# Nine chunks turned by TensorE, mask selections on GpSimd, and a rebuilt order in a gated-attention and feed-forward kernel

## The chip, the cores and the metric

The kernel runs on one core of a Trainium2 chip. Its time is the device time of one execution in microseconds. Five engines work on it, each through its own queue in order: TensorE (PE in the profile; its weight loads are PEld), VectorE (DVE), ScalarE (ACT), GpSimd (POOL) and SyncE (SP), which issues all DMAs here.

## What is computed

A gated linear attention runs over 768 steps for 4 batches of 8 heads of width 48; its outputs are the 3072 tokens of a feed-forward layer with a hidden width of 2048. The weights come as 64-bit floats.

```python
state = np.zeros((B, H, D, D), dtype=np.float32)
for t in range(S):
    state = alpha[:, :, t, :, None] * state + np.einsum('bhd,bhe->bhde', k[:, :, t], v[:, :, t])
    y[:, :, t] = np.einsum('bhd,bhde->bhe', q[:, :, t], state)
x = y.transpose(0, 2, 1, 3).reshape(B * S, H * D)
h = x @ w_in
g = np.where(h >= 1, h, np.where(h <= -1, 0.0, (h + 1) ** 2 / 4))
out = g @ w_out
```

## The kernel before

**Tiling.** The tokens are cut into 24 chunks of 128 (numbered from 0, six to a batch), and the chunks into eight groups of three. Attention works by chunk, the feed-forward layer by group. The 2048 hidden columns are 16 tiles of 128 (`f`); the weights of two tiles are a pair `u`, so there are eight pairs.

**Preparing a chunk** (`prepare`). Alpha, k and q are brought into a form with the head width on partitions ("turned"). For chunks below `EARLY` they are loaded as they lie, 192 KB each, and TensorE turns them into a bank of PSUM (L521); for the others four DMAs of 96 KB per tensor load them in a form that VectorE transposes (L534) into a tile `turn` in SBUF. From the turned alpha VectorE makes two scans, `Q` forward (L610) and `inv` backward (L636), after scaling four columns (L601). Then `inv` is multiplied by the turned k (L654) and `Q` by the turned q (L660). GpSimd does the latter for chunks below `HELP`, after ScalarE has copied the turned q out of PSUM (L658), and for chunks from `EARLY` on; VectorE does it for those between.

**Attending a chunk** (`attend`, `begin_chunk`, `follow`). TensorE transposes the K product (L681), makes scores (L696) and state updates (L709) in two banks of PSUM. The scores are masked in two halves, into `Q` and into `other` (L781 on VectorE). For chunks below `HELP` the second half is copied by ScalarE (L754) and multiplied by the mask on GpSimd (L760). VectorE adds the updates into the state (L736, L738). Then TensorE makes the outputs (L835), and ScalarE and VectorE write them as a high and a low part into `ring` (L859, L864). From chunk 7 on, the outputs of a chunk come right behind the scores of the next. From group 1 on, six DMAs move parts within `ring` (L880).

**The feed-forward layer** (`hidden`, `second`). For a group and a tile `f`, nine matmuls make the hidden values (L931); VectorE clips them (L975), ScalarE squares (L960), VectorE takes the maximum (L986), ScalarE and GpSimd split the result in a high and a low part (L990, L991), and nine matmuls multiply it with the second weights (L1009). Nine matmuls of L931 or of L1009 are called a block here; there are 256. The first two groups run over half of the tiles each, then over the other half; their partial sums go to memory and back.

**Decoding the weights** (`decode`). Each of the 16 weight tiles of 128x768 is made from its 64-bit form by two ScalarE passes (L354, L362), two on VectorE (L370, L381), an addition (L393) and, after a ScalarE copy (L404), a subtraction (L405). The last two may go to GpSimd or VectorE.

**The order** is set by `Plan.order`: every instruction has a duration and a due time (`key`), and an estimate of when its engine, operands and buffers are free; the planner takes them one after the other and so fixes each engine's queue, and which of two engines takes an instruction that has two ways. A chunk's due time is `due`, `MARGIN` ahead of the blocks that need it; loads are due `LOAD` and weight loads `FETCH` ahead, decodings `DECODE`. Where TensorE would wait in the first `WARMTH` us, the planner puts in filling matmuls (L1080), which compute nothing. Attention has three of the eight banks of PSUM from chunk `ROOM` on; the chunks below may use `FIRST`.

Of the kernel before, what the change touches and what calls it, by code (L numbers as in the profile page):

```python
# [15 lines left out]
ALU = mybir.AluOpType  # L16
# [11 lines left out]
SHARE = 2  # L28
EARLY = 7
MORE = 2  # L30
WARM = 20
LAG = 3.0
FETCH = 12.0
LOAD = 8.0
DECODE = 4.0
PREPARE = 2.5
MARGIN = 9.0
AHEAD = 12.0
FIRST = 6
ROOM = 4  # L40
LATER = 8.0
MERGE = 6
WARMTH = 60.0
HELP = 3
VHELP = 6
SPLIT = 0
CLIPS = 6.0
NEAR = 0.25

# [22 lines left out]
class Plan:  # L72
# [57 lines left out]
    def order(self):  # L130
        free = dict.fromkeys(("PE", "DVE", "ACT", "POOL", "SP"), 1.0)
        slots = {name: [(0.0, -i, None) for i in range(n)] for name, (n, share, _) in self.sizes.items() if share == name}
# [8 lines left out]
        ready = {}  # L141
# [3 lines left out]
        mode, wire, done, freed = None, 0.0, [], 0  # L145
# [81 lines left out]
def gated_attention_ffn(ctx: ExitStack, tc: tile.TileContext, q, k, v, alpha, w_in, w_out, out):  # L227
    nc = tc.nc
# [73 lines left out]
    with ExitStack() as main:  # L302
# [116 lines left out]
        def weights(u):  # L419
# [7 lines left out]
            size = P * NW * DM * (8 if wide else 4)  # L427
            fetch = key - FETCH
            for r in range(2):
# [31 lines left out]
            wo[u] = make([P, 2, NW, DM], F32R)  # L461
            decode(u, "i", ti, wi[u], "p k f -> p (k f)", key - DECODE)
            decode(u, "o", to, wo[u], "p j m -> p (j m)", key - DECODE + LAG)

# [12 lines left out]
        def load(x, j, key):  # L477
            b, t0 = j // PER, j % PER * CH
            t, rows = raws[x], {"a": alpha, "k": k, "q": q}[x][b, :, t0 : t0 + CH, :]
            if j < EARLY:  # L480
                if j < 2:
                    plan.op("POOL", 0.15, -99, lambda: nc.gpsimd.memset(whole(t, j)[:, :, D:], 1.0), [], [(x, j % 2)])
                plan.op(
# [28 lines left out]
        def turned(x, j, key, to=()):  # L512

            t = raws[x]
            if j < EARLY:
# [10 lines left out]

                flips[j] = plan.op("PE", 0.45, key, flip, [(x, j % 2)], [ps, *to], mode="full", after=[flips[j]] if j in flips else [])
                return ps, view
# [16 lines left out]
        def prepare(j, key):  # L545
# [109 lines left out]
            qt, qT = turned("q", j, key + 0.2)  # L655
            if j < HELP:
                qs = buf("tp", "turn", [P, G * CH], 2)
                plan.op("ACT", 0.55, key + 0.2, lambda qT=qT: nc.scalar.copy(out=qs(), in_=qT()), [qt], [qs])  # L658
                qt, qT = qs, lambda: qs()
            mul = lambda e: e.tensor_tensor(out=flat(Q()), in0=flat(Q()), in1=qT(), op=ALU.mult)  # L660
            in_ps = HELP <= j < EARLY
            ways = [("DVE", 0.66, lambda: mul(nc.vector), not in_ps), ("POOL", 1.3, lambda: mul(nc.gpsimd), True)]
# [78 lines left out]
        def follow(j, key):  # L741
# [5 lines left out]
            for r, to in enumerate((Q, other)):  # L747
                for u in range(2):
                    if r and j < HELP:
# [9 lines left out]
                        if u:  # L759
                            cut = lambda e: e.tensor_tensor(  # L760
                                out=other()[0:HC].rearrange("p g (u t) -> p g u t", u=2),
                                in0=other()[0:HC].rearrange("p g (u t) -> p g u t", u=2),
                                in1=mask[0:HC, None, None, 0:HC].broadcast_to([HC, G, 2, HC]),
                                op=ALU.mult,
                            )
                            plan.op(
                                "POOL",
                                1.35,
                                key,
                                lambda: cut(nc.gpsimd),  # L770
                                [other],
                                [other],
                                port=True,
                                other=("DVE", 0.66, lambda: cut(nc.vector), True),
                            )
# [311 lines left out]
        for j in range(NCH):  # L1087
            n = max(n for n in range(NG) if first[n] <= j)
            since = begin[n - 1] if n > 0 else begin[n] - AHEAD
            due = since + (begin[n] - since) * (j - first[n] + 1) / groups[n] - MARGIN  # L1090
            prepare(j, due - PREPARE)
# [175 lines left out]
```

## Time and profile before

| | us |
|---|---|
| median of 3 runs (540.56 to 541.62) | 541.18 |
| the profiled execution | 542.22 |
| its span, first to last instruction | 540.4 |
| TensorE busy | 516.0 |
| VectorE busy | 399.3 |
| GpSimd busy | 276.0 |
| ScalarE busy | 265.5 |
| matmuls of L931 / L1009 / L1080 | 1152 / 1152 / 149 |

The page's slices show TensorE at nine tenths or more in every slice from 160 us on, and lower before. So the views that are used are those of the first 170 us. A row names the line, the engine, the operation and its tiles (out<-in); "idle before" is how long the engine stood idle and what released it.

### The profile page before, as it was taken

The page shows a single profiled execution, that of the slowest core. Times are in us where ns is not written, and L with a number is a line of the kernel's source. Part 1 is how long each engine was busy: PE and PEld are TensorE (multiplying, and loading weights), DVE is VectorE, ACT ScalarE, POOL GpSimd, SP SyncE. Part 2 cuts the span into 40 slices and gives each one's busy share as a digit, 9 for nine tenths or more (in the row PEclk, how much of TensorE's full clock was granted, in tenths as well). Part 3 has the DMA queues.
Part 4 walks back from the last instruction along what each step waited for, and adds up shares of the span by engine and source line. Part 5 has one row for each costly group of instructions (what it writes and reads, how often), then busy time and mean ns, then how long its engine had stood idle before and what let it go on. Part 6 is the DMA issues. An engine that isn't in the chain of part 4 may idle for free.

```text
span 540.4 us, 12713 instructions
## 1 busy us (share of the span) xinstructions
PE 516.0 (95%) x4923; PEld 494.9 (92%) x4923; DVE 399.3 (74%) x709; ACT 265.5 (49%) x490; POOL 276.0 (51%) x295
## 2 busy tenths in 40 slices
PE   8898979998589999999999999999999999999995
PEld 6787869987589999999999999999999999999995
DVE  4789889899988987967968887777787884334332
ACT  4668877676343444344354453444444544333332
POOL 7555888799955525425524543443543543233330
PEclk9989998999989999999999999999999999999999
DMA  9989699934044663334333444335324300101001
GB/s 178 196 173 225 146 210 197 268 74 118 7 111 134 146 154 90 87 79 122 86 77 96 102 105 106 100 61 140 96 45 116 90 16 3 22 1 44 2 0 49
DMA packets 109457, 55.05 MB, mean 102 GB/s; under 512 B 71536, under 2 KB 104272, under 8 KB 109392
## 3 DMA queue, kind: packets, MB, share of 16 engines
q1 hardware_dynamic: 109392, 54.19, 43.2%
q8 instruction: 40, 0.66, 0.5%
q14 instruction: 25, 0.20, 0.1%
HBM read 46.20 MB, written 5.90 MB: 96 GB/s over the span
## 4 chain that ended last, share of the span: by engine, by line
PE 79%; DVE 12%; issue 3%; ACT 2%; POOL 2%; DMA 1%; SPq 0%; DVEq 0%; ACTq 0%; POOLq 0%
PE ps L1009 33%; PE ps L931 33%; PE ps L835 5%; PE ps L709 2%; PE ps L681 2%; DVE w L381 2%; PE ps L1080 2%; PE ps L696 2%; DVE Q L610 2%; DVE inv L636 1%; DVE w L370 1%; DVE meet L649 1%; POOL wt L405 1%; DVE inv L654 1%; DVE gf L986 1%
## 5 line engine op out<-in xcount | busy, mean ns | idle before, releaser
L991 POOL TENSOR_TENSOR gh<-gf,gh 128x384 fp32r<-128x384 f32 x127 | 146.7, 1160 | 162.4 <-ACT gh L990 133.3
L1009 PE MATMUL ps<-wt,gh 128*128 128x384 f32 x1152 | 226.2, 341 | 2.1 <-POOL gh L991 2.1
L931 PE MATMUL ps<-ring,wt 128*128 128x384 f32 x1152 | 226.1, 343 | 1.9 <-POOL wt L405 1.8
L931 PEld LDWEIGHTS ps<-ring,wt 128*128 128x128 f32 x1152 | 205.3, 190 | 3.6 <-POOL wt L405 2.5
L1009 PEld LDWEIGHTS ps<-wt,gh 128*128 128x128 f32 x1152 | 202.9, 189 | 4.3 <-POOL gh L991 3.7
L960 ACT ACTIVATE gf<-gf,half_b 128x384 f32<-128x384 f32 x122 | 75.0, 616 | 114.3 <-DVE gf L975 90.9
L975 DVE TENSOR_SCALAR gf<-ps 128x384 f32<-128x384 f32 x122 | 67.0, 551 | 58.8 <-PE ps L931 50.1
L990 ACT CAST gh<-gf 128x384 fp32r<-128x384 f32 x128 | 65.7, 513 | 74.5 <-DVE gf L986 60.5
L986 DVE TENSOR_TENSOR gf<-gf,ps 128x384 f32<-128x384 f32 x128 | 70.0, 549 | 33.8 <-ACT gf L960 33.3
L728 ACT COPY both<-state 48x192 f32<-48x192 f32 x65 | 22.7, 350 | 45.4 <-POOL state L812 39.8
L405 POOL TENSOR_TENSOR wt<-w,wt 128x768 fp32r<-128x768 f32 x16 | 33.8, 2114 | 4.3 <-ACT wt L404 4.2
L393 POOL TENSOR_TENSOR w<-w,wt 128x768 int32<-128x768 int32 x14 | 27.4, 1960 | 10.1 <-DVE w L381 5.6
L660 POOL TENSOR_TENSOR Q<-Q,turn 128x512 f32<-128x512 f32 x20 | 25.8, 1292 | 7.2 <-DVE turn L534 5.9
L835 PE MATMUL ps<-other,both 128*64 128x64 f32 x372 | 27.9, 225 | 1.6 <-issue 1.5
L812 POOL TENSOR_TENSOR state<-state,last 128x192 f32<-128x192 f32 x20 | 11.3, 567 | 33.5 <-DVE state L738 33.4
L835 PE MATMUL ps<-Q,both 128*64 128x64 f32 x372 | 28.0, 226 | 0.1
L610 DVE TENSOR_TENSOR_SCAN Q<-turn,fwd 128x512 f32<-128x512 f32 x17 | 23.2, 1362 | 6.5 <-PE ps L835 6.4
L835 PEld LDWEIGHTS ps<-Q,both 128*64 128x64 f32 x372 | 24.0, 137 | 3.6 <-issue 1.5
L681 PE MATMUL ps<-ident,inv 128*128 128x128 f32 x96 | 15.2, 282 | 10.8 <-DVE inv L654 10.4
L781 DVE TENSOR_TENSOR Q<-ps,mask 64x256 f32<-64x256 f32 x48 | 20.3, 423 | 6.8 <-ACT other L746 5.3
L835 PEld LDWEIGHTS ps<-other,both 128*64 128x64 f32 x372 | 23.9, 137 | 1.1 <-issue 0.8
L681 PEld LDWEIGHTS ps<-ident,inv 128*128 128x128 f32 x96 | 11.7, 144 | 13.1 <-DVE inv L654 11.1
(89 smaller groups left out, 525.9 us busy)
## 6 DMA issues: line engine op xcount, KB each, us to landing
raw_a<-in_alpha SPq DMA_DIRECT2D x68, 96.0 KB, 2.4
raw_k<-in_k SPq DMA_DIRECT2D x68, 96.0 KB, 2.6
raw_q<-in_q SPq DMA_DIRECT2D x68, 96.0 KB, 2.3
wt<-in_moe_w_out SPq DMA_DIRECT2D x8, 768.0 KB, 9.8
vt<-in_v SPq DMA_DIRECT2D x24, 192.0 KB, 3.1
wt<-in_moe_w_in SPq DMA_DIRECT2D x16, 288.0 KB, 7.3
out<-ot SPq DMA_DIRECT2D x24, 192.0 KB, 2.4
both<-in_v SPq DMA_DIRECT2D x72, 48.0 KB, 2.4
```

The source lines that it names most:

```text
L393: add = lambda e: e.tensor_tensor(out=bits(), in0=bits(), in1=word(I32, 0), op=ALU.add)
L405: sub = lambda e: e.tensor_tensor(out=part(1), in0=data(), in1=part(0).bitcast(F32), op=ALU.subtract)
L610: lambda: nc.vector.tensor_tensor_scan(flat(Q()), aT(), flat(fwd), 0.0, ALU.mult, ALU.max),
L681: nc.tensor.transpose(out=kp()[:, g], in_=K()[:, g], identity=ident)
L835: nc.tensor.matmul(out=ps()[halves[r], to, halves[u]], lhsT=lhsT[:, u, r], rhs=x()[:, g, halves[u]], start=m + u == 0, stop=True, skip_gro ...
L931: nc.tensor.matmul(out=h(), lhsT=win(f, w)[:, kt], rhs=ring[:, at, kt, a, :], start=(m == 0), stop=(m == 3 * KT - 1),)
L960: lambda: nc.scalar.activation(out=gf(), in_=in_(), func=func, scale=scale, bias=bias),
L975: lambda: nc.vector.tensor_scalar(out=gf(), in0=h(), scalar1=-1.0, scalar2=1.0, op0=ALU.max, op1=ALU.min),
L986: lambda: nc.vector.tensor_tensor(out=gf(), in0=gf(), in1=h(), op=ALU.max),
L990: plan.op("ACT", 0.08 + 0.41 * w, key + 0.4, lambda: nc.scalar.copy(out=gh()[:, 0], in_=gf()), [gf], [gh])
L991: sub = lambda e: e.tensor_tensor(out=gh()[:, 1], in0=gf(), in1=gh()[:, 0].bitcast(F32), op=ALU.subtract)
L1009: nc.tensor.matmul(out=o_ps[seg][t](), lhsT=gh()[:, a, (t - c0) * CH : (t - c0 + 1) * CH], rhs=wout(f, w), start=(f == f0 and i == 0), sto ...
```

## The change

The chunks turned by TensorE (`EARLY`) are nine instead of seven. The Q product by way of ScalarE and GpSimd gets a limit of its own, `QHELP`, which is 0, so that VectorE makes it from PSUM for all nine. The masking of the second half by ScalarE and GpSimd holds for chunks below 4 instead of 3, and GpSimd does it by a selection (`affine_select`) instead of a product with the mask, which VectorE could take over before and now cannot. The due times of the first two groups have margins of their own, the first weight pair is fetched and decoded earlier than the others relative to its use, and several other numbers of the planner differ. The memsets of padding no longer stand in the way of the loads in the planner's account. From these the planner makes another order for all engines.

```diff
-EARLY = 7
+EARLY = 9
...
-LOAD = 8.0
-DECODE = 4.0
+LOAD = 6.0
+DECODE = 3.0
 PREPARE = 2.5
-MARGIN = 9.0
-AHEAD = 12.0
-FIRST = 6
-ROOM = 4
-LATER = 8.0
+MARGIN = 11.0
+MARGIN0 = 9.0
+MARGIN1 = 6.0
+FETCH0 = 18.0
+DECODE0 = 4.0
+AHEAD = 20.0
+FIRST = 5
+ROOM = 2
+LATER = 4.0
...
-HELP = 3
+QHELP = 0
+HELP = 4
...
-NEAR = 0.25
+NEAR = 0.0
...
-            fetch = key - FETCH
+            fetch = key - (FETCH if u else FETCH0)
+            ready = key - (DECODE if u else DECODE0)
...
-            if j < HELP:
+            if j < QHELP:
...
-            in_ps = HELP <= j < EARLY
+            in_ps = QHELP <= j < EARLY
...
-                            cut = lambda e: e.tensor_tensor(
-                                out=other()[0:HC].rearrange("p g (u t) -> p g u t", u=2),
-                                in0=other()[0:HC].rearrange("p g (u t) -> p g u t", u=2),
-                                in1=mask[0:HC, None, None, 0:HC].broadcast_to([HC, G, 2, HC]),
-                                op=ALU.mult,
-                            )
...
+                                lambda: nc.gpsimd.affine_select(
+                                    out=other()[0:HC].rearrange("p g (u t) -> p g u t", u=2),
+                                    in_=other()[0:HC].rearrange("p g (u t) -> p g u t", u=2),
+                                    compare_op=ALU.is_ge,
+                                    fill=0.0,
+                                    base=0,
+                                    pattern=[[0, G], [0, 2], [1, HC]],
+                                    channel_multiplier=-1,
+                                ),
...
-            due = since + (begin[n] - since) * (j - first[n] + 1) / groups[n] - MARGIN
+            due = since + (begin[n] - since) * (j - first[n] + 1) / groups[n] - (MARGIN, MARGIN0, MARGIN1)[n + 1 if n < 2 else 0]
```

In after the lines of the instructions are 6 or 7 higher: L521 is L527, L660 is L666, L681 is L687, L931 is L938, L1009 is L1016.

Three places show how the queues move. First TensorE, before, from the first block on, which stands behind chunk 3's outputs (`ps` is PSUM, `ring` the attention's outputs, `wt` weights):

```order
L931 MATMUL ps<-ring,wt 128x384 x9
L681 MATMUL ps<-ident,inv 128x128 x4
L696 MATMUL ps<-Q,inv 64x64 x16
L709 MATMUL ps<-vt,ks 64x48 x16
L521 MATMUL ps<-ident,raw_a 128x128 x4
L931 MATMUL ps<-ring,wt 128x384 x9
L521 MATMUL ps<-ident,raw_k 128x128 x4
L521 MATMUL ps<-ident,raw_q 128x128 x4
```

In after, TensorE at the same chunks (the block of L938 ahead of chunk 4's outputs is the fourth):

```order
L1016 MATMUL ps<-wt,gh 128x384 x9
L527 MATMUL ps<-ident,raw_k 128x128 x4
L527 MATMUL ps<-ident,raw_q 128x128 x4
L938 MATMUL ps<-ring,wt 128x384 x9
L687 MATMUL ps<-ident,inv 128x128 x4
L702 MATMUL ps<-Q,inv 64x64 x16
L938 MATMUL ps<-ring,wt 128x384 x9
L715 MATMUL ps<-vt,ks 64x48 x8
L527 MATMUL ps<-ident,raw_a 128x128 x4
L527 MATMUL ps<-ident,raw_k 128x128 x4
L527 MATMUL ps<-ident,raw_q 128x128 x4
L1016 MATMUL ps<-wt,gh 128x384 x18
```

By the end of chunk 5's outputs ten blocks stand in the queue now, where two stood, and there are 93 filling matmuls in all instead of 149.

Second VectorE at chunk 8, before, up to its K product (`turn` is a tile turned by VectorE, `gf` belongs to the feed-forward layer):

```order
L986 TENSOR_TENSOR gf<-gf,ps 128x384
L610 SCALAR_TENSOR_TENSOR Q<-turn,fwd 128x512
L614 RECIPROCAL bwd<-Q 128x4
L628 COPY inv<-bwd 128x1
L975 TENSOR_SCALAR gf<-ps 128x384
L636 SCALAR_TENSOR_TENSOR inv<-turn,bwd 128x511
L534 STREAM_TRANSPOSE turn<-raw_q 128x4x4x32
L986 TENSOR_TENSOR gf<-gf,ps 128x384
L649 TENSOR_TENSOR meet<-fwd,inv 128x4
L654 TENSOR_TENSOR inv<-inv,turn 128x512
```

In after, VectorE at the same chunk:

```order
L607 TENSOR_SCALAR fwd<-ps 128x4
L613 MEMSET ps 128x4
L616 SCALAR_TENSOR_TENSOR Q<-ps,fwd 128x512
L620 RECIPROCAL bwd<-Q 128x4
L634 COPY inv<-bwd 128x1
L642 SCALAR_TENSOR_TENSOR inv<-ps,bwd 128x511
L655 TENSOR_TENSOR meet<-fwd,inv 128x4
L660 TENSOR_TENSOR inv<-inv,ps 128x512
```

The transposes are gone, the scans read PSUM, and no piece of the feed-forward layer stands between them.

Third TensorE ahead of chunk 8's K transposition, before:

```order
L1009 MATMUL ps<-wt,gh 128x384 x18
L931 MATMUL ps<-ring,wt 128x384 x9
L1009 MATMUL ps<-wt,gh 128x384 x9
L931 MATMUL ps<-ring,wt 128x384 x9
L1009 MATMUL ps<-wt,gh 128x384 x9
L931 MATMUL ps<-ring,wt 128x384 x18
L681 MATMUL ps<-ident,inv 128x128 x4
```

In after, TensorE at the same place:

```order
L527 MATMUL ps<-ident,raw_a 128x128 x4
L527 MATMUL ps<-ident,raw_k 128x128 x4
L1016 MATMUL ps<-wt,gh 128x384 x9
L938 MATMUL ps<-ring,wt 128x384 x9
L527 MATMUL ps<-ident,raw_q 128x128 x4
L1016 MATMUL ps<-wt,gh 128x384 x9
L938 MATMUL ps<-ring,wt 128x384 x9
L687 MATMUL ps<-ident,inv 128x128 x4
```

Chunk 8's three turns now stand among the blocks; 39 blocks are ahead of its K transposition instead of 44, and 51 ahead of chunk 9's instead of 54.

## Rows read from the trace of the kernel before

**Rows 1.** Stretches: us, busy time of each engine, clock, DMA share, GB/s.

```profile
52.00:104.00 52.00, 48.02 (x391) 44.65 (x392) 45.65 (x67) 39.02 (x68) 44.64 (x33) 0.93 0.90 196
104.00:164.00 60.00, 50.30 (x441) 47.98 (x440) 54.08 (x75) 34.46 (x59) 47.80 (x33) 0.94 0.39 98
200.00:500.00 300.00, 299.99 (x2773) 293.85 (x2773) 216.63 (x402) 131.20 (x251) 125.07 (x136) 1.00 0.32 77
```

**Rows 2.** Waits of TensorE in the first 164 us: total, times, longest.

```profile
PE ps L681 <- DVE inv L654: 10.4, 5, 6.9
```

**Rows 3.** TensorE in order of time: start, us, instructions, count, idle before.

```profile
19.37 0.66 PE L521 MATMUL ps<-ident,raw_a 128*128 128x128 f32 x4
...
20.74 1.36 PE L1080 MATMUL ps<-zeros 128*128 128x256 bf16 x11
...
62.90 1.82 PE L1009 MATMUL ps<-wt,gh 128*128 128x384 f32 x9
...
150.06 1.12 PE L681 MATMUL ps<-ident,inv 128*128 128x128 f32 x4 [6.95 <-DVE inv L654]
...
164.10 3.34 PE L931 MATMUL ps<-ring,wt 128*128 128x384 f32 x18
...
170.45 0.60 PE L681 MATMUL ps<-ident,inv 128*128 128x128 f32 x4
```

**Rows 4.** VectorE in order of time, from chunk 8's K product to chunk 9's.

```profile
148.56 1.45 DVE L654 TENSOR_TENSOR inv<-inv,turn 128x512 f32<-128x512 f32 x1
...
151.45 0.54 DVE L370 TENSOR_SCALAR w<-w 128x768 int32<-128x768 int32 x1
152.03 0.96 DVE L381 SCALAR_TENSOR_TENSOR w<-wt,w 128x768 int32<-128x768 int32 x1
...
168.09 0.69 DVE L654 TENSOR_TENSOR inv<-inv,turn 128x512 f32<-128x512 f32 x1
```

**Rows 5.** VectorE by line and form, first 160 us: count, busy us, mean ns, idle.

```profile
L381 DVE SCALAR_TENSOR_TENSOR w<-wt,w 128x768 int32<-128x768 int32 x16 | 21.5, 1346 | 0.3
L370 DVE TENSOR_SCALAR w<-w 128x768 int32<-128x768 int32 x16 | 13.5, 845 | 2.1 <-ACT w L354 2.1
L986 DVE TENSOR_TENSOR gf<-gf,ps 128x384 f32<-128x384 f32 x24 | 13.0, 547 | 3.8 <-ACT gf L960 3.6
...
L636 DVE TENSOR_TENSOR_SCAN inv<-ps,bwd 128x511 f32<-128x511 f32 x7 | 8.9, 1271 | 0.0
L610 DVE TENSOR_TENSOR_SCAN Q<-ps,fwd 128x512 f32<-128x512 f32 x7 | 8.6, 1224 | 0.2
...
L781 DVE TENSOR_TENSOR other<-ps,mask 64x256 f32<-64x256 f32 x12 | 5.1, 421 | 0.3
...
L654 DVE TENSOR_TENSOR inv<-inv,ps 128x512 f32<-128x512 f32 x7 | 4.8, 686 | 0.6
L610 DVE TENSOR_TENSOR_SCAN Q<-turn,fwd 128x512 f32<-128x512 f32 x2 | 4.7, 2341 | 0.0
L393 DVE CUSTOM_DVE_ANT_0 w<-wt,w 128x1536 uint16<-128x1536 uint16 x2 | 4.3, 2128 | 0.0
L636 DVE TENSOR_TENSOR_SCAN inv<-turn,bwd 128x511 f32<-128x511 f32 x2 | 4.1, 2057 | 0.0
...
L534 DVE STREAM_TRANSPOSE turn<-raw_a 128x512 f32<-128x512 f32 x3 | 3.4, 1129 | 0.0
L654 DVE TENSOR_TENSOR inv<-inv,turn 128x512 f32<-128x512 f32 x2 | 2.9, 1454 | 0.1
L660 DVE TENSOR_TENSOR Q<-Q,ps 128x512 f32<-128x512 f32 x4 | 2.7, 677 | 0.0
...
L601 DVE TENSOR_SCALAR fwd<-turn 128x4 f32<-128x4 f32 x2 | 1.6, 798 | 0.0
...
L601 DVE TENSOR_SCALAR fwd<-ps 128x4 f32<-128x4 f32 x7 | 1.1, 158 | 5.6 <-PE ps L521 5.6
```

**Rows 6.** GpSimd by line and form in the first 160 us, columns as in rows 5.

```profile
L405 POOL TENSOR_TENSOR wt<-w,wt 128x768 fp32r<-128x768 f32 x16 | 33.8, 2114 | 4.3 <-ACT wt L404 4.2
```

## What the prediction says

> **What bounds the kernel now.** I read the stretches first. From 200 to 500 us TensorE is busy for 299.99 of 300 us at a granted clock of 1.00, so nothing that another engine does there can show in the time. From 52 to 104 it is busy for 48.0 of 52 us at 0.93, and from 104 to 164 for 50.3 of 60 us at 0.94, while VectorE is busy for 45.7 and 54.1 us, more than TensorE in the second stretch [rows 1]. So the loss is early, and what matters is when TensorE gets into its unbroken part. The waits say on whom it waits: 10.4 us of K transpositions (L681) for the product `inv` that VectorE makes at L654, 6.9 us of it at once [rows 2]. That one is chunk 8's: the product ends at 150.01 us [rows 4] and the K transposition starts at 150.06 [rows 3]. Chunk 9's product ends at 168.78, and its K transposition starts at 170.45 without a wait.
>
> I use this last point as the mark. From it to the end are 540.4 - 170.45 = 369.95 us of a TensorE that never waits. In the order of before, 54 of the 256 feed-forward blocks (nine matmuls each, L931 or L1009) stand ahead of it. Four blocks take 170.45 - 164.10 = 6.35 us, so 1.587 us each [rows 3]. In the order of after, 51 blocks stand ahead of chunk 9's K transposition; the other three come behind it, and the rest of the work behind it is the same: 369.95 + 3 x 1.587 = 374.7 us. So the span after is t9 + 374.7, with t9 the start of chunk 9's K transposition. The whole question is t9.
>
> **The change, part by part: VectorE's queue up to chunk 9's product.** I counted VectorE's instructions ahead of that product in both orders and priced what differs.
> - Chunks 7 and 8 are turned by TensorE: six VectorE transposes of 1.13 us go, -6.78 [rows 5].
> - For these two chunks the first scaling, the two scans and the K product now read PSUM. Before, they took 0.798, 2.341, 2.057 and 1.454 us on average for a turned tile in SBUF; from PSUM the same four took 0.158, 1.224, 1.271 and 0.686 [rows 5]. Twice the difference of 3.31 is -6.62.
> - The Q product (L660) of chunks 0, 1, 2, 7 and 8 comes from GpSimd to VectorE, 0.677 us each: +3.39 [rows 5].
> - Two masks of chunk 3 leave VectorE: 2 x 0.42 = -0.84 [rows 5].
> - Of the weight decoding, one addition of 2.13 us goes back to GpSimd [rows 5], and two subtractions (L405) come to VectorE. The trace shows none of these there. The nearest rows are one-input and two-input passes over 128x768: 0.54 us for the fastest [rows 4], 1.346 for the mean of the two-input ones [rows 5]. I bound one by 0.54 and by twice that mean, 2.7, and take 1.35, as it has two inputs in SBUF like L381. Sum +0.57.
> - One product of the feed-forward (L986) less stands ahead, -0.55 [rows 5].
>
> The sum is -10.83, and 168.78 - 10.83 = 157.9 us. A second effect: the weight passes L370 and L381 took 0.845 and 1.346 us on average, and 0.54 and 0.96 where GpSimd was quiet [rows 4, 5], which is 16 x (0.305 + 0.386) = 11 us of slowdown. GpSimd's own load from 52 to 164 us, 92.4 us [rows 1], loses two subtractions of 2.11 [rows 6] and two Q products and gains one addition of about 2: some 5%. I take 5% of 11, -0.6, and t9 from VectorE is 157.3.
>
> **TensorE's own side.** Could it be ready by then? Before, it reached chunk 8's K transposition at 150.06 - 6.95 = 143.1 [rows 3]. The order of after has five blocks fewer ahead of it (-7.9), six turns more (three took 20.74 - 19.37 = 1.37 us, so +2.7), and 93 filling matmuls instead of 149 (eleven took 1.36 us, so 56 x 0.124 = -6.9) [rows 3]: 131.0. VectorE's product for chunk 8 by the same count (no Q product of chunk 8 yet, 2.2 for one decoding less, 3.3 for three blocks less, one more copy out at 0.55) is due at 150.01 - 15.9 - 0.6 = 133.5. So a wait stays there, 2.5 us where 6.95 were. From chunk 8's K transposition to chunk 9's took 20.4 us with ten blocks; with twelve, 23.6 at most: 157.1. Both engines arrive at 157, and t9 = 157.3.
>
> Costed at nothing: six turns later on (they are counted above); ScalarE's three copies of turned Q less and two score copies more, since ScalarE is not in the waits of TensorE for chunk 8 or 9; four mask selections on GpSimd for three mask products. No such selection of 512 columns is in the trace; at GpSimd's two-input rate of 2.11 us for 768 columns [rows 6] it is bounded by 1.4 us, about what the mask product may cost, and by nothing from below. The cover is that in these 40 us VectorE, not GpSimd, is ahead of TensorE; without it the fourth one costs up to 1.4 us. The first weights are fetched ahead of chunk 2's inputs: 1.57 MB at the 196 GB/s of the stretch from 52 to 104 us [rows 1] is 8 us. With the eight input tensors ahead, 1.57 MB too, chunk 2's alpha lands after 17 us and some start-up; TensorE turned it at 19.37 before [rows 3], and VectorE now has three more pieces ahead of it (a decoding and two Q products). If that cover fails, each us late is a us on t9. On SP's queue the pair moves of group 1 (L880) now stand ahead of the last three weight pairs, not four; the weights of the last pair are needed only by the 23rd block of L931, which stands behind chunk 8's K transposition, at 133.5 us or later, and hides it.
>
> **The sum.** 157.3 + 374.7 = 532.0, against 540.4 in the profiled execution: -8.4 us. That execution took 542.22 with what lies around the span, 1.04 over the median of 541.18. Taken off the median: **532.8 us**.
>
> By pace: before, the 46 blocks from the first of L1009 at 62.90 us to 164.10 came at 2.2 us each [rows 3]. The order of after has 48 from its first of L1009 to t9, 105.6 us at this pace, so that one has to start at 51.7 us. It stands behind chunk 4's update there, and behind chunk 5's outputs before.
>
> **Two rules of the Trainium skill.** Rows 5 show scans reading PSUM directly, and the order of after has the same form for chunks 7 and 8, with no copy. The Trainium skill, TensorE: Matmul & The Clock Gate, Part 4: PE-mode transpose, says that a transpose on TensorE ends in PSUM "so you need a DVE copy after". By that, six copies of about 0.68 us would take 4.1 us back, and the time would be 536.9; by the rows it is 532.8, and the rows hold since the consumers themselves read PSUM.
> Rows 4 and 5 show L381, two inputs in SBUF, at 0.96 and at 1.346 on average. The Trainium skill, SBUF - State Buffer, Who interferes with whom, says that a VectorE instruction with two SBUF inputs contends with a GpSimd instruction that reads SBUF, and that the later one waits in full. By that, each of the two subtractions now on VectorE could wait a whole GpSimd subtraction: an estimate of 3.1 us each instead of 1.35, and 536.3 in all. The range holds it.
>
> **The rivals.**
> - *TensorE takes over.* The wait for VectorE at chunks 8 and 9 goes wholly, because slowdowns by GpSimd fall more than 5%. For it: all 11 us of them stand on VectorE ahead of t9. Then TensorE's 131.0 + 22 holds, and with the other 3.5 us of waits for `inv` gone too [rows 2], t9 is 149.5 to 153: 525 to 528.5.
> - *No gain.* The first blocks start sooner but the loop from L931 over VectorE, ScalarE and GpSimd to L1009 keeps its pace of 2.2 us and starts late, at 59 us instead of 51.7: 59 + 105.6 = 164.6, and the time is 540. For it: VectorE has 4.2 us more ahead of chunk 4's product than before (two decodings at 1.5, three Q products at 0.68, two masks less). Against it: a first block no longer waits for chunk 5.
> - *Slower: turns wait for a bank.* The turns of chunks 7 and 8 stand between blocks on TensorE's queue, and each needs one of the three PSUM banks that attention has; they wait for VectorE to read one empty, and all blocks behind them wait too. At one scan each (1.25 us) six turns cost 7.5 us, all of the gain; from 1.5 us each it is slower than before. At a scan and its neighbours, 2.5 us, 15 us come on and some 3.5 of the waits go: 544. Against it: before, the turns of chunks 2 to 6 stood in the same way and do not appear in the waits [rows 2].
> - *The order does not hold.* The planner's times miss the slowdowns, and a late weight or input stops all engines in the rebuilt order: 541 to 543.
>
> **How the numbers follow.** Forecast 0.60 (529 to 537), TensorE takes over 0.13, no gain 0.12 (537 to 541), slower by banks 0.10, the order does not hold 0.05. The bounds of the subtractions (-1.7 to +2.7), of the slowdowns (0 to -5) and of the selections give 526 to 537 for the forecast's own case. The range 524 to 540 leaves out the slower cases and half of the no-gain case. About 0.2%, 1.1 us, is what a measurement of this kernel can tell from no change. Faster by more: 0.60 + 0.13 + 0.07 = 0.80; same 0.07; slower 0.13.
>
> **What would show it.** Right: chunk 9's K transposition (L687 in after) at 154 to 160 us, with 374 to 376 us behind it; waits of L687 for `inv` of 2 to 6 us instead of 10.4; scans of chunks 7 and 8 at 1.2 to 1.3 us; no turn (L527) in the waits of TensorE for over 2 us in all; filling matmuls 93. The subtraction on VectorE at 0.9 to 2.7 us. Wrong: idle time of TensorE after t9, which would mean that the attention behind it now comes late; waits of L527 for VectorE; a first block of L1016 later than 56 us.

## The result and the profile after

The changed kernel takes 534.81 us in the median of four runs (534.15 to 535.24), beside 541.4 for the kernel before in four runs; the ratio is 0.988 (95% interval 0.986 to 0.990). The profiled execution took 535.24 with a span of 533.1, 7.3 us under the span before. Forecast were 532.8 and a span of 532.0; so 6.6 us are gained where 8.4 were forecast.

The stretches after (columns as in [rows 1]):

```profile
52.00:104.00 52.00, 45.88 (x408) 42.08 (x407) 45.88 (x78) 39.57 (x68) 37.93 (x32) 0.97 0.73 154
104.00:164.00 60.00, 56.70 (x550) 52.76 (x550) 51.43 (x86) 36.04 (x64) 45.28 (x37) 1.00 0.53 131
200.00:500.00 300.00, 300.00 (x2774) 294.49 (x2773) 201.99 (x386) 127.74 (x244) 117.41 (x143) 1.00 0.30 73
```

The late part was full before and is full now. The gain is in the stretch from 104 to 164 us: TensorE is busy for 56.7 us instead of 50.3, and its clock is granted whole instead of at 0.94. From 52 to 104 us it is even busy for 2 us less.

TensorE in order of time after, with the first block of L1016 and the K transpositions (L687) of chunks 8 and 9:

```profile
49.78 1.95 PE L1016 MATMUL ps<-wt,gh 128*128 128x384 f32 x9
...
135.85 0.65 PE L687 MATMUL ps<-ident,inv 128*128 128x128 f32 x4 [0.17 <-DVE inv L660]
...
158.86 0.63 PE L687 MATMUL ps<-ident,inv 128*128 128x128 f32 x4 [0.21 <-DVE inv L660]
```

The wait of 6.95 us ahead of chunk 8's K transposition [rows 3] is 0.17 us now. The mark t9 is 158.86, and 374.2 us lie behind it (forecast 157.3 and 374.7).

The waits of TensorE after, first 164 us (in all, times, longest):

```profile
PE ps L527 <- issue: 3.1, 1, 3.1
PE ps L687 <- DVE inv L660: 2.5, 5, 1.0
PE ps L715 <- ACT ks L690: 2.0, 2, 1.4
PE ps L938 <- DVE ring L871: 2.0, 1, 2.0
```

Waits for `inv` fell from 10.4 us [rows 2] to 2.5. A new one heads the list: a turn (L527).

### The profile page after: what moved, and what is told of

Same layout as the page of the kernel before. It is cut to its first block, busy times and chain, and to the rows that moved or that the text cites. A ratio compares the mean times of both kernels' runs of the same rounds, so it can differ in the third digit from the quotient of the medians.

```text
span 533.1 us, 12597 instructions
## 1 busy us (share of the span) xinstructions
PE 510.2 (96%) x4891; PEld 488.2 (92%) x4891; DVE 378.4 (71%) x703; ACT 262.5 (49%) x487; POOL 256.1 (48%) x296
## 4 chain that ended last, share of the span: by engine, by line
PE 80%; DVE 9%; POOL 3%; issue 3%; ACT 2%; DMA 1%; SPq 1%; DVEq 0%; POOLq 0%; ACTq 0%
PE ps L1016 36%; PE ps L938 35%; PE ps L842 3%; PE ps L715 2%; PE ps L687 2%; POOL w L398 2%; PE ps L702 2%; DVE inv L642 1%; DVE Q L616 1%; POOL gh L998 1%; DMA vt<-in_v 1%; DVE w L386 1%; SPq L493 1%; POOL wt L410 1%; DVE w L375 1%
## 5 line engine op out<-in xcount | busy, mean ns | idle before, releaser
L1016 PE MATMUL ps<-wt,gh 128*128 128x384 f32 x1152 | 226.4, 341 | 3.9 <-POOL gh L998 1.8
L938 PE MATMUL ps<-ring,wt 128*128 128x384 f32 x1152 | 225.3, 341 | 2.8 <-DVE ring L871 2.0
L998 POOL TENSOR_TENSOR gh<-gf,gh 128x384 fp32r<-128x384 f32 x127 | 137.0, 1079 | 175.9 <-ACT gh L997 150.1
L1016 PEld LDWEIGHTS ps<-wt,gh 128*128 128x128 f32 x1152 | 202.2, 188 | 7.0 <-POOL gh L998 3.5
L938 PEld LDWEIGHTS ps<-ring,wt 128*128 128x128 f32 x1152 | 203.6, 188 | 5.2 <-DVE ring L871 2.4
L398 POOL TENSOR_TENSOR w<-w,wt 128x768 int32<-128x768 int32 x15 | 29.2, 1948 | 12.7 <-PE ps L1016 4.4
L410 POOL TENSOR_TENSOR wt<-w,wt 128x768 fp32r<-128x768 f32 x14 | 27.2, 1946 | 0.2
L690 ACT COPY ks<-ps 128x512 f32<-128x512 f32 x24 | 14.0, 585 | 25.6 <-PE ps L687 25.6
L819 POOL TENSOR_TENSOR state<-state,last 128x192 f32<-128x192 f32 x20 | 12.4, 618 | 28.8 <-DVE state L744 26.7
L616 DVE TENSOR_TENSOR_SCAN Q<-turn,fwd 128x512 f32<-128x512 f32 x15 | 18.7, 1249 | 5.8 <-PE ps L842 5.8
L734 ACT COPY both<-state 48x192 f32<-48x192 f32 x52 | 18.2, 349 | 8.8 <-DVE state L744 4.9
L666 POOL TENSOR_TENSOR Q<-Q,turn 128x512 f32<-128x512 f32 x15 | 19.4, 1295 | 6.1 <-DVE turn L540 5.7
L386 DVE SCALAR_TENSOR_TENSOR w<-wt,w 128x768 int32<-128x768 int32 x16 | 19.7, 1233 | 0.2
```

The costliest lines, as they stand in the source:

```text
L386: lambda: nc.vector.scalar_tensor_tensor(out=bits(), in0=word(I32, 1), scalar=-0x80000000, in1=bits(), op0=ALU.bitwise_and, op1=ALU.bitwis ...
L398: add = lambda e: e.tensor_tensor(out=bits(), in0=bits(), in1=word(I32, 0), op=ALU.add)
L410: sub = lambda e: e.tensor_tensor(out=part(1), in0=data(), in1=part(0).bitcast(F32), op=ALU.subtract)
L616: lambda: nc.vector.tensor_tensor_scan(flat(Q()), aT(), flat(fwd), 0.0, ALU.mult, ALU.max),
L938: nc.tensor.matmul(out=h(), lhsT=win(f, w)[:, kt], rhs=ring[:, at, kt, a, :], start=(m == 0), stop=(m == 3 * KT - 1),)
L998: sub = lambda e: e.tensor_tensor(out=gh()[:, 1], in0=gf(), in1=gh()[:, 0].bitcast(F32), op=ALU.subtract)
```

## The experiments

Executions of one kernel scatter by 1 to 6 us. So medians and ratios to the kernel before on the same chip decide, and a profile shows where time lies; a span is 1.7 to 2.1 us under its execution's time. "t9" is the start of chunk 9's K transposition. Theory A is the prediction's: VectorE's queue sets t9. For a changed number the planner makes another order, so such a run shows the number together with its order; only extra scans and filling matmuls leave the order as it is.

### The change, part by part

**Only the turning**: the kernel before with one number changed.

```diff
-EARLY = 7
+EARLY = 9
```

> The kernel before with nine early chunks (EARLY = 9) and nothing else; its order is that of before up to chunk 6 (149 filling matmuls, first block of L1009 behind chunk 5's outputs), and 55 blocks instead of 54 stand ahead of chunk 9's K transposition, so 369.95 - 1.59 = 368.4 us behind it. Theory A, VectorE's queue alone sets that point: priced by the rows of before, the work ahead of chunk 9's product falls by 8.6 us, t9 is 161 to 162, the span 530 (as good as all of the change). Theory B, TensorE's own queue is next (six turns more, no fill less): it is ready for chunk 8's K transposition at 143.1 - 1.6 + 2.7 = 144.2 us, VectorE's product is there at 141.4, and 12 blocks later t9 is 167.8: span 536, and K transpositions L681 wait for inv under 2 us. Theory C, the early start of the first blocks is the gain and turning is not: t9 stays near 170, span 538.5 to 540.5.

Measured: 536.88 us, ratio 0.992 (0.989 to 0.995). TensorE in order of time, the K transpositions of chunks 8 and 9:

```profile
141.80 0.60 PE L681 MATMUL ps<-ident,inv 128*128 128x128 f32 x4
...
163.65 0.60 PE L681 MATMUL ps<-ident,inv 128*128 128x128 f32 x4
```

VectorE in order of time, the product that the second one needs:

```profile
156.72 0.69 DVE L654 TENSOR_TENSOR inv<-inv,turn 128x512 f32<-128x512 f32 x1
```

Theory C, that the early start is the gain and turning is not, falls: turning alone gives 4 to 5 us. VectorE is done at 157.4 us, 6.2 before TensorE gets there, and neither K transposition waits. So theory B holds in kind: TensorE is the later one at t9. Its 167.8 was too late by 4. TensorE came to chunk 8's K transposition 2.4 us before the 144.2 reckoned, which stays unexplained. From there to chunk 9's it took 21.85 us for the twelve blocks, where 23.6 had been reckoned from before; 1.9 us of the 23.6 were a clock at half, as the runs on the clock show below.

**All but the turning**: the changed kernel with

```diff
-EARLY = 9
+EARLY = 7
```

> The changed kernel with seven early chunks as before (EARLY = 7), everything else of the change kept; its order is that of after up to chunk 6, with 93 filling matmuls, and 51 blocks ahead of chunk 9's K transposition, so 374.7 us behind it. Theory A, VectorE's queue: its work ahead of chunk 9's product is only 1.6 us less than in before, t9 is 167 to 168.5, the span 541.5 to 543, and L687 waits for inv by over 8 us: the rest of the change is worth nothing without the turning. Theory C, the early start is the gain: t9 is 160 to 163, the span 535 to 537.

Measured: 544.41 us, ratio 1.005 (1.003 to 1.007), slower than before. TensorE in order of time:

```profile
139.75 1.11 PE L687 MATMUL ps<-ident,inv 128*128 128x128 f32 x4 [3.78 <-DVE inv L660]
...
167.30 0.60 PE L687 MATMUL ps<-ident,inv 128*128 128x128 f32 x4
```

And the wait of L687 in the first 172 us:

```profile
PE ps L687 <- DVE inv L660: 8.1, 5, 3.8
```

Theory A had t9 at 167 to 168.5, 374.7 us behind it and over 8 us of waits; it is 167.30, 374.9 and 8.1. The new due times are a loss while VectorE still transposes chunks 7 and 8: three blocks fewer (4.8 us) stand ahead of t9, and t9 comes only 3.15 us earlier than in before.

**All but the masks and Q products**: the changed kernel with

```diff
-QHELP = 0
-HELP = 4
+QHELP = 3
+HELP = 3
...
-                                lambda: nc.gpsimd.affine_select(
...
+                                lambda: cut(nc.gpsimd),
...
+                                other=("DVE", 0.66, lambda: cut(nc.vector), True),
```

> The changed kernel with the masks of chunks 0 to 2 as a product on GpSimd again, chunk 3's masks on VectorE, and the Q products of chunks 0 to 2 back on GpSimd behind a copy by ScalarE; the due times and the nine early chunks stay. 50 blocks ahead of chunk 9's K transposition, so 376.3 us behind it, and 114 filling matmuls instead of 93. Theory A, VectorE's queue: its work ahead of chunk 9's product is 2.1 us less than in after, t9 is 156.5 to 157.5, the span 532.5 to 534, no worse than after. Theory B, TensorE: 21 fills more (2.6 us) and one block less (1.6 us) make t9 160, the span 536. That masks and Q products were a gain of their own would show as a span over 537.

Measured: 535.19 us, ratio 0.988 (0.985 to 0.991), the same as the changed kernel; t9 is at 157.21, with a span of 533.5. Theory A had 156.5 to 157.5 and 532.5 to 534. The K transposition waits 1.35 us there for VectorE's product: TensorE, with one block less ahead, is early, and that gains nothing. Masks and Q products are worth nothing that can be measured here, with intervals of 0.3%.

**All but the due times**: the changed kernel with the planner's numbers of before.

```diff
-MARGIN = 11.0
+MARGIN = 9.0
...
-MARGIN1 = 6.0
-FETCH0 = 18.0
+MARGIN1 = 9.0
+FETCH0 = 12.0
...
-AHEAD = 20.0
-FIRST = 5
-ROOM = 2
-LATER = 4.0
+AHEAD = 12.0
+FIRST = 6
+ROOM = 4
+LATER = 8.0
...
```

> The changed kernel with the planner's numbers of before (LOAD 8, DECODE 4, one margin of 9, AHEAD 12, FIRST 6, ROOM 4, LATER 8, NEAR 0.25, GpSimd free from 1 us); nine early chunks, masks and Q products stay as in after. 55 blocks ahead of chunk 9's K transposition, so 368.4 us behind it, and 126 filling matmuls. Theory A, VectorE's queue: 6.1 us less ahead of chunk 9's product than in before, t9 is 162.7, the span 531. Theory B, TensorE: ready for chunk 8's K transposition at 141.3, 12 blocks later t9 is 165, the span 533.3. Theory C, the rebuilt order with its earlier first block is the gain: t9 167 to 170, the span 536 to 539.

Measured: 537.23 us, ratio 0.992 (0.989 to 0.995), as with the turning alone. t9 is 166.28 without a wait, and the span 535.0. Both lie between theory B (165 and 533.3) and theory C (167 to 170, 536 to 539). TensorE's waits in the first 172 us show what B left out, blocks and turns that wait for VectorE:

```profile
PE ps L938 <- DVE gf L993: 3.4, 1, 3.4
PE ps L527 <- DVE gf L993: 2.7, 1, 2.7
```

The four ratios make a small table:

| | chunks 7 and 8 on VectorE | turned by TensorE |
|---|---|---|
| due times of before | 1 (the kernel before) | 0.992 (masks old or new) |
| due times of after | 1.005 (masks new) | 0.988 (masks old or new) |

Turning gives 0.8% with the old due times and 1.7% with the new ones; the new due times cost 0.5% without it and give 0.4% with it, with intervals of 0.2 to 0.3%. Which of the planner's numbers gives the 0.4% was not taken apart, and its account of the padding memsets was not varied alone.

### Which engine is behind at t9

Three kernels move VectorE's work there. In two of them, the changed kernel and the one with only the turning, chunk 9's backward scan is made four times, which writes the same values again and leaves every engine's order as it is.

```diff
-                lambda: nc.vector.tensor_tensor_scan(
+                lambda: [nc.vector.tensor_tensor_scan(
...
-                ),
+                ) for _ in range(4 if j == 9 else 1)],
```

> The changed kernel with the backward scan of chunk 9 (L642) made four times in place of once; the other instructions and the order of all engines stay. In after the product behind it ends at 158.7 us and chunk 9's K transposition starts at 158.86 with a wait of 0.21. Three scans at 1.28 to 1.5 us are 3.8 to 4.5 us. Theory A, VectorE's queue reaches TensorE here: all but some tenths arrive, t9 is 162.5 to 163.3, the span 536.7 to 537.5 (+3.6 to +4.4). Theory B, TensorE alone bounds the changed kernel and VectorE has slack: the span moves by under 1 us.

Measured: 541.0 us, ratio 1.0005 (0.998 to 1.003), 6.5 us over the changed kernel in the profiled spans (539.6). TensorE in order of time:

```profile
162.64 1.09 PE L687 MATMUL ps<-ident,inv 128*128 128x128 f32 x4 [4.17 <-DVE inv L660]
163.38 3.23 PE L938 MATMUL ps<-ring,wt 128*128 128x384 f32 x9
166.41 2.76 PE L1016 MATMUL ps<-wt,gh 128*128 128x384 f32 x9
```

t9 moves by 3.78 us, as A says; B falls. But the end moves by 6.5, more than either had. The blocks behind the wait are slow, and that is taken up below.

> The kernel before with nine early chunks (as e1_only_turning) with the same three extra scans in chunk 9. In e1_only_turning chunk 9's product ends at 157.4 us and its K transposition starts at 163.65, so VectorE is 6.2 us ahead there. Theory B, TensorE has taken over in that kernel: the added 3.8 to 4.5 us vanish, the span stays at 533.7 within 1 us, and t9 starts without a wait. Theory A, VectorE's queue sets t9 in it: the span is 537 to 538.

Measured: 541.61 us, ratio 1.001 (0.9995 to 1.003), against 0.992 without the scans: 4 to 5 us worse. Theory B, which had the scans vanish in VectorE's 6.2 us of lead, falls; the span of 539.6 is above theory A's 538 too. The K transposition starts without a wait, at 167.62, but the blocks around it do wait. The stretch of 27 us from 157 us in this kernel:

```profile
157.00:184.00 27.00, 24.75 (x219) 22.72 (x218) 23.67 (x40) 9.92 (x19) 10.51 (x11) 1.00 0.42 108
```

and the like stretch, as far from t9, of the one without the scans:

```profile
153.00:180.00 27.00, 27.00 (x240) 26.52 (x238) 22.41 (x45) 11.88 (x23) 11.81 (x14) 1.00 0.52 133
```

TensorE loses 2.25 of 27 us in five waits of 0.3 to 0.5 us, of which the kernel without the scans has none there. One is for a maximum (`gf`, L986) that VectorE makes right behind the scans, at 162.43 us, three are for `gh`, which is made from such maxima, and one is for a move within `ring`. That all five come of the scans is read from the order of the queues; the rest of the 4 to 5 us was not traced. (The profiled span, 539.6, is also 2.4 us late already at chunk 8's K transposition, ahead of the scans; that part is scatter, so the median is the better size.) VectorE's lead at one product was no slack of its whole queue.

In the third, the changed kernel turns chunk 9 by TensorE as well.

```diff
-EARLY = 9
+EARLY = 10
```

> The changed kernel with ten early chunks (EARLY = 10): chunk 9 is turned by TensorE too. 50 blocks instead of 51 stand ahead of chunk 9's K transposition (376.3 us behind it, and three turns of it taken out of what is behind), and VectorE's work ahead of chunk 9's product falls by 7.2 us by the rows. Theory A, VectorE's queue alone: t9 is 152, the span 528 to 529. Theory D, both engines arrive together in the changed kernel, so relieving VectorE alone gives nothing and the three turns are paid on TensorE: t9 157 to 158.5, the span 533 to 535, and no wait of L687 for inv over 0.5 us at chunk 9.

Measured: 537.22 us, ratio 0.9935 (0.992 to 0.995), some 2.5 us slower than the changed kernel. VectorE's product for chunk 9 ends at 156.8 us and t9 is 157.93, without a wait. Theory A's 528 falls, theory D's 157 to 158.5 holds. The busy time up to that product (the third engine in the row is VectorE):

```profile
0.00:156.84 156.84, 139.56 (x1557) 126.69 (x1558) 128.01 (x224) 105.32 (x188) 108.82 (x122) 0.97 0.71 154
```

Of the 7.2 us of VectorE's work that were to go only 3.2 went (131.23 in the changed kernel), and the product comes 1.9 us earlier. TensorE is 0.9 us earlier at t9, with a block less ahead of it, and is now the later one: this relief of VectorE, smaller than the theories had it, buys nothing more, and the three turns are paid.

### The clock behind a wait

In two kernels a long wait of TensorE is filled with matmuls that compute nothing, in the bank that the K transposition then overwrites.

```diff
             def turn_keys():
+                for _ in range(50 if j == 8 else 0):
+                    nc.tensor.matmul(out=flat(kp())[:, 0:256], lhsT=zeros, rhs=nothing, start=True, stop=True)
```

> The kernel before with 50 filling matmuls of 256 columns put ahead of chunk 8's K transposition, into the bank that it then overwrites; they fit into its wait of 6.95 us for VectorE (50 at 0.107 to 0.124 us are 5.3 to 6.2 us), and nothing else moves. Theory K, a long wait of TensorE costs its own length and then a granted clock of half for some us: in before the K transposition behind the wait took 1.12 us where 0.60 is usual, and the block behind it 3.16 where 1.74 is usual, 1.9 us together; with TensorE busy in the wait these come back, the span is 538.5 and the median 0.35% under that of before. Theory N, the clock has no part in it: within 0.1%.

Measured: 540.17 us, ratio 0.998 (0.9965 to 0.9997), span 538.2. TensorE in order of time:

```profile
142.14 5.63 PE L681 MATMUL ps<-zeros 128*128 128x256 bf16 x50
149.25 0.66 PE L683 MATMUL ps<-ident,inv 128*128 128x128 f32 x4 [1.47 <-DVE inv L654]
149.66 1.82 PE L1011 MATMUL ps<-wt,gh 128*128 128x384 f32 x9
```

Behind the wait of the kernel before, the K transposition took 1.12 us [rows 3], and the block after it

```profile
150.83 3.16 PE L1009 MATMUL ps<-wt,gh 128*128 128x384 f32 x9
```

Here they take 0.66 and 1.82. The clock (third figure from the right) was granted at half in before and is whole here; before and with the fills:

```profile
150.00:153.00 3.00, 2.94 (x11) 2.94 (x12) 2.97 (x7) 1.72 (x3) 0.00 (x0) 0.50 0.65 203
```

```profile
149.25:151.00 1.75, 1.75 (x12) 1.75 (x13) 1.75 (x4) 1.31 (x3) 0.00 (x0) 1.00 0.89 269
```

Theory K's mechanism is there; its size is 0.2% in the medians where 0.35% was expected.

In the other one the scans of chunk 9 stay, with `32 if j == 9` fills.

> The kernel of e5_delay_after (three extra scans in chunk 9, span 539.6, 6.5 us over after for 3.9 us of scans) with 32 filling matmuls ahead of chunk 9's K transposition, in the wait of 4.17 us that the scans make (32 at 0.107 to 0.124 us are 3.4 to 4.0). Theory K, the part over 3.9 us is a clock granted at half behind the wait (K transposition 1.09 instead of 0.63 us, the two blocks behind it 3.23 and 2.76 instead of 1.84 and 1.73, 2.9 us together): the span is 536.7 to 537, t9's K transposition takes 0.60. Theory Q, the part over 3.9 us comes from what stands behind the scans on VectorE's queue: the span stays at 539 to 540.

Measured: 539.14 us, ratio 0.996 (0.995 to 0.998), 0.4% better than with the scans alone; span 535.4, 1.3 us under what theory K had. TensorE in order of time:

```profile
157.14 3.67 PE L687 MATMUL ps<-zeros 128*128 128x256 bf16 x32
161.37 0.66 PE L689 MATMUL ps<-ident,inv 128*128 128x128 f32 x4 [0.56 <-DVE inv L660]
161.78 1.84 PE L940 MATMUL ps<-ring,wt 128*128 128x384 f32 x9
```

From t9 to the end are 374.0 us, as in the changed kernel (374.2), where it was 377.0 without the fills. So 2.8 to 3.0 us of the loss were the clock in these profiles, and theory Q falls. By the ratios of the medians the fills give back 0.4%, 2.2 us; what stays lost against the changed kernel on the same chip (535.25) is 3.9 us, about the scans alone.

### A faster order

The turn that waits 3.1 us in the changed kernel, and both engines arriving together at t9, leave TensorE's early idle time as what can still be won. A third set of planner's numbers, which puts 54 blocks instead of 51 ahead of chunk 9's K transposition:

```diff
-LAG = 3.0
+LAG = 3.5
...
-DECODE = 3.0
+DECODE = 2.5
...
-MARGIN = 11.0
-MARGIN0 = 9.0
+MARGIN = 9.0
+MARGIN0 = 10.0
 MARGIN1 = 6.0
-FETCH0 = 18.0
-DECODE0 = 4.0
+FETCH0 = 20.0
+DECODE0 = 6.0
...
-ROOM = 2
+ROOM = 4
...
-MERGE = 6
+MERGE = 7
...
-QHELP = 0
+QHELP = 1
...
-VHELP = 6
+VHELP = 5
...
```

> The changed kernel with other planner's numbers (ROOM 4, FETCH0 20, QHELP 1, VHELP 5, MARGIN 9, MARGIN0 10, DECODE0 6, DECODE 2.5, LAG 3.5, MERGE 7), a try for a faster order. 54 blocks instead of 51 stand ahead of chunk 9's K transposition, so 369.95 us behind it; 94 filling matmuls; first block of L1016 behind chunk 3's outputs instead of chunk 4's. VectorE's work ahead of chunk 9's product is 1.4 us more than in after, so by theory A t9 is 160.2 and the span 530. Theory D, TensorE's queue is as much a bound: three blocks more come to 158.9 + 4.8 = 163.6, less what the earlier first block saves of idle time (0 to 3 us): span 531 to 533.6. If the numbers carry no gain beyond those of after, 534 or more.

Measured: 533.67 us, ratio 0.987 (0.985 to 0.989); its five executions lie between 528.95 and 534.04, and the profiled one, with a span of 527.2, is the lowest. Since this does not tell it apart from the changed kernel, both ran again on one chip.

> The changed kernel once more, beside e12_joint_again on the same chip: 533.1 of span and 0.988 of before.

> The kernel of e8_joint_due_times once more, for a comparison with the changed kernel on the same chip. In e8_joint_due_times the median was 0.9869 of before against 0.9879 for the changed kernel elsewhere, and the profiled span 527.2. If TensorE's earlier start of the blocks (54 instead of 51 ahead of chunk 9's K transposition at the same t9) is a gain, the median is 1 to 4 us under that of the changed kernel; if the profiled execution was only a lucky one, within 1 us.

Measured: 535.25 us (534.21 to 536.78), ratio 0.989 (0.987 to 0.991), for the changed kernel, and 532.65 (531.73 to 533.7), ratio 0.9845 (0.982 to 0.987), for the new order. No execution of the one lies among those of the other; the new order is 2.6 us faster, the fastest kernel here. Its chunk 9 in order of time:

```profile
161.43 0.60 PE L687 MATMUL ps<-ident,inv 128*128 128x128 f32 x4
```

and that of the changed kernel beside it:

```profile
159.32 0.63 PE L687 MATMUL ps<-ident,inv 128*128 128x128 f32 x4 [0.21 <-DVE inv L660]
```

The new order is 2.1 us later at t9 but three blocks (4.8 us) further. The turn's wait of 3.1 us is gone from its waits, and three of 5.8 us in all, for VectorE's scans (L642), head them. Which of its numbers makes the gain was not taken apart.

## Why the prediction was right, step by step

**The mark.** What lies behind t9, by counted blocks, held to 0.5 us in four orders: 374.2 us against 374.7 in after, 374.9 against 374.7 without the turning, 376.3 against 376.3 with the old masks, 368.7 against 368.4 with the old due times. It was 1.6 us more than counted with the turning alone (370.0 against 368.4), 1.5 more with ten early chunks (376.4 against 376.3 less three turns of 1.4 us in all), and 1.4 less with the new order (368.6 against 369.95); what makes these three differ was not traced. A wait at t9 itself broke it (377.0 with the scans), by the clock.

**VectorE's work** ahead of chunk 9's product was to fall by 10.83 + 0.6 = 11.4 us. Busy time of before up to the end of that product, and of after:

```profile
0.00:168.78 168.78, 149.97 (x1610) 136.61 (x1611) 142.96 (x233) 107.49 (x191) 126.49 (x132) 0.95 0.72 158
```

```profile
0.00:158.71 158.71, 141.41 (x1560) 126.69 (x1560) 131.23 (x230) 106.84 (x192) 110.09 (x122) 0.98 0.74 160
```

142.96 to 131.23 is -11.73. The terms, from VectorE by line and form in the first 160 us of after:

```profile
L386 DVE SCALAR_TENSOR_TENSOR w<-wt,w 128x768 int32<-128x768 int32 x16 | 19.7, 1233 | 0.2
...
L375 DVE TENSOR_SCALAR w<-w 128x768 int32<-128x768 int32 x16 | 13.9, 871 | 2.3 <-ACT w L359 2.2
L642 DVE TENSOR_TENSOR_SCAN inv<-ps,bwd 128x511 f32<-128x511 f32 x9 | 11.4, 1272 | 0.0
L616 DVE TENSOR_TENSOR_SCAN Q<-ps,fwd 128x512 f32<-128x512 f32 x9 | 11.0, 1223 | 0.3
...
L410 DVE TENSOR_TENSOR wt<-w,wt 128x768 fp32r<-128x768 f32 x2 | 2.2, 1125 | 0.2 <-ACT wt L409 0.2
```

All nine scans from PSUM take 1.22 and 1.27 us, as taken. The subtraction is 1.125, taken as 1.35 between 0.54 and 2.7. The slowdown of the two weight passes against their quiet 0.54 and 0.96 is 16 x (0.331 + 0.273) = 9.7 us instead of 11, so 1.4 less where 0.6 had been taken. The selection on GpSimd, bounded by nothing and 1.4 us, took 0.66:

```profile
L770 POOL TENSOR_SCALAR_AFFINE_SELECT other<-other 64x512 f32<-64x512 f32 x4 | 2.6, 658 | 1.1 <-ACT other L760 1.1
```

Two things that the sum did not have went the other way: chunk 9's own scaling and forward scan took 0.88 and 1.51 us instead of 0.23 and 1.22, and the ten small products of L655 took 0.8 us more in all. So it is partly luck that the sum was met to 0.3 us: terms that were off by 0.5 to 0.9 us offset each other.

**Where t9 was missed by 1.6 us.** Not in VectorE's work but in its idle time, 25.8 us before and 27.5 after up to that product; the prediction held it constant. Its largest part after, in VectorE's waits of the first 158.7 us:

```profile
DVE gf L993 <- ACT gf L967: 9.7, 6, 2.8
```

It was 3.6 us for the 24 such instructions of before [rows 5]; other waits of VectorE shrank. What made it grow was not tested.

**TensorE's own side** was the weakest step. It was to be ready for chunk 8's K transposition at 131.0, and was there at 135.7. Busy time of before up to the like point, and of after (TensorE comes first):

```profile
0.00:143.11 143.11, 131.24 (x1429) 118.39 (x1429) 120.42 (x197) 97.88 (x173) 111.49 (x120) 0.96 0.78 169
```

```profile
0.00:135.68 135.68, 118.85 (x1352) 105.47 (x1352) 110.35 (x192) 95.03 (x171) 93.54 (x108) 0.97 0.80 169
```

131.24 to 118.85 is -12.4, where the sum had -12.1. What failed is the idle time, which the sum held constant: it rose from 11.9 to 16.8 us. The longest new wait is of the kind that the prediction priced as the rival "turns wait for a bank", for chunks 7 and 8: they do not wait for VectorE, but a turn of chunk 6 does. TensorE in order of time after:

```profile
66.12 0.66 PE L527 MATMUL ps<-ident,raw_a 128*128 128x128 f32 x4
69.84 1.09 PE L527 MATMUL ps<-ident,raw_k 128*128 128x128 f32 x4 [3.07 <-issue]
70.72 1.06 PE L527 MATMUL ps<-ident,raw_q 128*128 128x128 f32 x4
71.44 4.21 PE L1016 MATMUL ps<-wt,gh 128*128 128x384 f32 x18
```

and VectorE:

```profile
63.81 2.50 DVE L386 SCALAR_TENSOR_TENSOR w<-wt,w 128x768 int32<-128x768 int32 x1
66.45 1.53 DVE L398 CUSTOM_DVE_ANT_0 w<-wt,w 128x1536 uint16<-128x1536 uint16 x1
68.01 0.86 DVE L788 TENSOR_TENSOR Q<-ps,mask 64x256 f32<-64x256 f32 x2
68.89 0.86 DVE L788 TENSOR_TENSOR other<-ps,mask 64x256 f32<-64x256 f32 x2
```

Two of attention's three banks hold chunk 5's scores and one the turned alpha; the masks that empty the scores stand behind two passes of the decoding, and the turn starts when the last mask ends, at 69.75. The first of the passes took 2.50 us instead of its quiet 0.96; an addition of GpSimd (L398) ran beside it from 63.45 to 65.50. The trace names no releaser, so this is read from the times and the code. The wait accounts for 3.1 of the 5.0 us of new idle time; the rest lies in shorter waits (L938 for `ring` 2.0, L715 for `ks` 0.9 more than before), less what the waits for `inv` gave back. The kernel without the turning has the same wait, 3.08 us at chunk 6, so it comes with the new due times and not with the turns that were added. No run took it out alone. Of the signs set down beforehand, this one came out wrong: turns wait for 4.5 us in all, where 2 was the bound.

**Both engines together.** The prediction had VectorE and TensorE meet at 157, and they meet at 158.7 to 158.9, from other sums: at chunk 8 TensorE was to wait 2.5 us for a product due at 133.5, and both were there at 135.7. That they meet so near to 157 is partly luck. More scans (+6.5 us), ten early chunks (no gain) and the turning alone (TensorE later) show each side. "TensorE takes over" (0.13) was near in kind: it is what the turning alone does. "No gain" (0.12), by a late first block, is shown by no run: without the turning the first block is early, and the loss is waits for VectorE.

**Pace.** "By pace the first block has to start at 51.7" was met (49.78), but it was no support: with the turning alone that block starts at 61.11 and 4 to 5 us are gained; without the turning it starts at about 51 and nothing is.

**The two rules.** The copy behind a transpose on TensorE (the Trainium skill, TensorE: Matmul & The Clock Gate, Part 4: PE-mode transpose), by which the time would be 536.9, is not there: the nine scans of each kind read PSUM. The rule on contention, by which each subtraction could take 3.1 us, did not strike VectorE's subtractions so (1.29 and 0.96 us). Beside the second of them GpSimd's own, which began 0.02 us later, took 2.65 us where 1.84 is usual:

```profile
122.36 0.96 DVE L410 TENSOR_TENSOR wt<-w,wt 128x768 fp32r<-128x768 f32 x1 [0.23 <-ACT wt L409]
```

```profile
122.38 2.65 POOL L410 TENSOR_TENSOR wt<-w,wt 128x768 fp32r<-128x768 f32 x1
```

So the price fell on GpSimd's instruction, the later of the two; below it falls on VectorE's.

## What to carry to other kernels

Fix a point behind which the bounding engine never waits, count the work that each order puts ahead of it, and ask when each engine gets there; that gave the span of the changed kernel to 1.1 us. Such a count leaves out idle time, which was off by 1.7 us on VectorE and 5.0 us on TensorE here. A relief on one engine and an earlier schedule can pay more together (1.2% here) than apart (0.8% and -0.5%), so test them in a two by two table. A lead at one product need not be slack of the queue: what stands behind the delayed instruction is late too.

## What the runs showed of the hardware that was not expected

**A wait is paid twice.** Behind a wait of 4.17 us the granted clock is half for some 6 us. The stretch of 6 us behind it in the kernel with the scans:

```profile
163.00:169.00 6.00, 6.00 (x22) 5.85 (x20) 4.57 (x9) 2.50 (x5) 2.25 (x2) 0.53 0.42 133
```

The mean of 0.53 is the lower of the two levels, 1.2 GHz, for nearly all of it. The Trainium skill, TensorE: Matmul & The Clock Gate, Terms, prices such time at its length times the missing share of the clock, an estimate of 6.0 x 0.47 = 2.8 us here; the runs agree, with 2.8 to 3.0 us regained by the fills in the profiles (2.2 in the medians). The prediction had no such term. In the kernel before it was 1.9 us behind chunk 8's wait, by its rows, and 1.1 us in the medians.

**A small instruction waits for a large one.** VectorE's L655, four columns wide, ran beside a subtraction of GpSimd. VectorE after:

```profile
57.17 1.81 DVE L655 TENSOR_TENSOR meet<-fwd,inv 128x4 f32<-128x4 f32 x1
```

and GpSimd:

```profile
57.12 1.84 POOL L410 TENSOR_TENSOR wt<-w,wt 128x768 fp32r<-128x768 f32 x1
```

Both end at 58.97, give or take 0.01; at 73.29 us the same instruction takes 0.17. The Trainium skill, SBUF — State Buffer, Who interferes with whom, has the later of two such instructions wait in full, and this pair agrees with it, at ten times the small one's own time.
